# Attention scores from quarters of the array, x kept in token rows: one change to a fused attention, expert and mixing kernel

## The chip, the cores and the metric

The kernel runs on one core of a Trainium2 chip. The metric is the device time of one execution in microseconds (us); lower is better. Engine names: PE is TensorE (matmuls; PEld its weight loads), DVE is VectorE, ACT is ScalarE, POOL is GpSimd, SP is SyncE, which issues nearly all DMAs here.

## What is computed

Three layers run one after another on two sequences of 768 tokens. The change lies in the first. Its reference, cut to what matters:

```python
B, H, S, D = 2, 8, 768, 64                       # block 32, window 16
k_sum = k.reshape(B, H, 24, 32, D).max(axis=3)   # 24 block maxima of k
v_sum = v.reshape(B, H, 24, 32, D).mean(axis=3)  # 24 block means of v
scores_l = scale * (q @ k.T)                     # kept where |i - j| < 16
scores_s = scale * (q @ k_sum.T) + log(32)
a = softmax(concat(masked scores_l, scores_s))
x = a @ concat(v, v_sum)                         # then (B, S, H * D)
```

Then each token is sent to one of 8 experts (512 to 1024 to 512, the choice partly carried over from the token before), and a last layer mixes tokens and channels.

## The kernel before, in words

**Units.** Heads are taken in pairs: n = 0..7 is a pair of a batch (four pairs to a batch). Queries are taken in windows of 64 tokens; window t needs the 96 keys around it and the 24 block maxima, KC = 120 columns. A unit k = 3n + g is four windows of one pair, so there are 24 units, k0 to k23. `units` is run by one loop (L907), whose body writes each engine's order out by hand; nothing is reordered later.

**One unit.** `attn_s` (L238) makes the scores: four fp32 matmuls of 128 rows by 128 columns, each over 120 moving columns. The 128 rows hold 64 channels of each of the two heads, and the stationary operand is `qb`, in which q stands twice on a diagonal with zeros elsewhere, so that the first 64 outputs belong to head 0 and the last 64 to head 1. `q_diag` (L207) copies q into it, on POOL for every pair but the first. Each fp32 matmul appears in the trace as two passes. The scores of a unit fill one PSUM bank of `sps`, with two banks in turn. DVE then adds the mask and takes the row minimum (L248, four instructions and their accumulator reads), and ACT takes the exponential (L250). In the next turn of the loop `attn_t` (L254) transposes the four results on PE, ACT copies them out (L258), later `attn_v` (L260) multiplies them with v in 64-column halves, and `attn_n` (L271) divides on DVE.

**Operands.** `ka[n]` holds the 120 score columns: `k_windows` (L218) copies the overlapping windows, `k_max` (L227) makes the block maxima on DVE and copies them to all 12 windows. For n = 0 ACT and DVE do this, for n = 1 DVE, then POOL. `kc[n]`, `qf[n]` and `vall` come by DMA in the order in which SP issues them; `kc` has two buffers, `qf` borrows two buffers of the expert stage. `vsum` (L174) makes the block means of v: matmuls at k3, k5 and k6 (batch 0), a copy by ACT (L181), a matmul (L184), a copy of one window by ACT (L192), and then POOL spreads it over the other 11 windows (L193, L195). The first `attn_v` stands in k9 and needs them.

**Behind the attention.** From k12 the finished rows of x are stored (`store_x`, L280) and transposed for the gate (`gate_T`, L288, L298; ACT copies them out, L304). In k17 the gate of batch 0 is computed (L316), and from k18 to k23 the routing of batch 0 (`route0`) runs in small DVE steps between the attention's, with some PE hops (L322, L350, L355, L371, L454). Then come the end of batch 1, the first gather of tokens and the expert layers (from L633), and from about 249 us the mixing layer.

The columns of x stand with all even heads first (`xs` is [64 h + i, window, pair, channel]), and the host permutes the rows of the gate's and the experts' first weights to match.

Of the kernel before, what the change touches and what calls it, by code (L numbers as in the profile page):

```python
# [10 lines left out]
F32 = mybir.dt.float32  # L11
F32R = mybir.dt.float32r
# [5 lines left out]
ALU = mybir.AluOpType  # L18
AX = mybir.AxisListType
PSUM = bass.MemoryType.PSUM  # L20
DRAM = bass.MemoryType.DRAM

B, H, S, D = 2, 8, 768, 64
NP = H // 2
NT = S // 64
DM = 512
E = 8
DFF = 1024
W = 96
NB = 24  # L30
KC = W + NB
D1 = D + 1
# [3 lines left out]
TS = 256  # L36
# [19 lines left out]
def consts():  # L56
    import numpy as np

    c = np.zeros((128, C_N), np.float32)
    p = np.arange(128)  # L60
    c[:, C_W8:C_W8 + 8] = 8 - np.arange(8)
    c[:, C_I128:C_I128 + 128] = np.arange(128)
    c[:, C_I26:C_I26 + 26] = np.arange(26)
    c[:, C_TOK:C_TOK + 12] = 128 * np.arange(12)[None, :] + p[:, None] + 1
    c[:, C_PAD:C_PAD + 30] = B * S + 1 + 128 * np.arange(30)[None, :] + p[:, None]
    s = 128 * np.arange(6)[None, :] + p[:, None]
    c[:, C_KEY:C_KEY + 6] = 16 * (s + 1)
    c[:, C_S0:C_S0 + 6] = s == 0
    c[:, C_TRI:C_TRI + 128] = p[:, None] < p[None, :]
    for x in range(3):  # L70
        c[16:48, C_IND + 34 * x] = 1.0 / 32
        c[48:80, C_IND + 34 * x + 1] = 1.0 / 32
    c[:, C_I13:C_I13 + 13] = np.arange(13)
    for x in range(4):
        for j in range(6):
            c[32 * x + j, C_PRM + 6 * x + j] = 1.0
    m = np.full((128, 3, KC), -1.0e9, np.float32)
    i = p % 64
    j = np.arange(W)
    band = np.abs(j[None, :] - 16 - i[:, None]) < 16  # L80
    for v, (lo, hi) in enumerate(((16, W), (0, W), (0, W - 16))):
        ok = band & (j >= lo)[None, :] & (j < hi)[None, :]
        m[:, v, :W][ok] = 0.0
        m[:, v, W:] = 8.0 * math.log(32.0)
    return c, m.reshape(128, 3 * KC)
# [3 lines left out]
def tile_attn_moe_mix(ctx: ExitStack, tc: tile.TileContext, qT, kT, vp, gw, w1, w2, wth, wtok, wch, cst, msk, out):  # L89
    nc = tc.nc  # L90
    V, A, G, T, SP = nc.vector, nc.scalar, nc.gpsimd, nc.tensor, nc.sync

    def pool(name, bufs, stack=ctx, **kw):
        kw.setdefault("reuse_waits", "tile")
        return stack.enter_context(tc.tile_pool(name=name, bufs=bufs, **kw))
# [3 lines left out]
    xd = dram.tile([B * S, DM], F32, name="xd")  # L99
# [5 lines left out]
    idn = const.tile([128, 128], F32, name="idn")  # L105
# [39 lines left out]
    xp = pool("xp", 1, sA)  # L145
    kp = pool("kp", 2, sA)
    ptp = pool("ptp", 1, sA)
    qp = pool("qp", 1, sA)
    psS = pool("psS", 2, sA, space=PSUM)
    psT = pool("psT", 2, sA, space=PSUM)  # L150
    psO = pool("psO", 2, sA, space=PSUM)

    qb = [qp.tile([128, NT, 128], F32, name=f"qb{i}") for i in range(2)]
    xs = [xp.tile([128, NT, NP, 64], F32, name=f"xs{1 - b}") for b in range(B)][::-1]
    ka, kcs = {}, {}
    qf = {}

# [8 lines left out]
    def vslot(b, g):  # L166
        return (3 * b + g) % NVS
# [33 lines left out]

    def load_q(n):
        b, p = divmod(n, NP)
        qf[n] = xt_p.tile([128, 4, TS], F32R, name="qf", tag="xl" if n % 2 else "xh").bitcast(F32).rearrange("p c t -> p (c t)")[:, 0:S]
        SP.dma_start(qf[n], qT[b, 2 * p:2 * p + 2].rearrange("h d s -> (h d) s"))

    def q_diag(n, lo, hi):  # L207
        for h in range(2):
            dst = qb[n % 2][64 * h:64 * h + 64, lo:hi, 64 * h:64 * h + 64]
            src = qf[n][64 * h:64 * h + 64].rearrange("p (t i) -> p t i", i=64)[:, lo:hi, :]  # L210
            if n > 0:
                G.tensor_copy(dst, src)
            elif h == 0:
                A.copy(dst, src)  # L214
            else:
                V.tensor_copy(dst, src)

    def k_windows(n):  # L218
        kc = kcs[n]
        ka[n] = kp.tile([128, NT, KC], F32, name="ka", tag="ka")  # L220
        win = bass.AP(tensor=kc.tensor, offset=kc.offset, ap=[list(kc.ap[0]), [64, NT], [1, W]])
        if n == 0:
            A.copy(ka[n][:, :, 0:W], win)
        else:
            (V if n < 2 else G).tensor_copy(ka[n][:, :, 0:W], win)

    def k_max(n, lo, hi):  # L227
        if lo == 0:
            kss[n] = st.tile([128, NB], F32, name="ks", tag="ks", bufs=2)
        V.tensor_reduce(kss[n].rearrange("p (c x r) -> p x c r", c=4, x=3)[:, lo:hi],  # L230
                        kcs[n][:, 16 + 256 * lo:16 + 256 * hi].rearrange("p (x c r j) -> p x c r j", c=4, r=2, j=32),
                        axis=AX.X, op=ALU.max)
        if hi == 3:
            (V if n < 2 else G).tensor_copy(ka[n][:, :, W:KC], kss.pop(n).unsqueeze(1).to_broadcast([128, NT, NB]))

    kss = {}

    def attn_s(n, g):  # L238
        sps = psS.tile([128, 4, KC], F32, name="sps", tag="s")
        for c in range(4):  # L240
            t = 4 * g + c
            T.matmul(sps[:, c, :], qb[n % 2][:, t, :], ka[n][:, t, :], start=True, stop=True)  # L242
        neg = sp.tile([128, 4, KC], F32, name="neg", tag="neg")
        mn = st.tile([128, 4], F32, name="mn", tag="mn")
        for c in range(4):
            t = 4 * g + c
            v = 0 if t == 0 else (2 if t == NT - 1 else 1)
            V.tensor_tensor_reduce(out=neg[:, c, :], in0=sps[:, c, :], in1=mk[:, v, :], scale=-0.125, scalar=3.0e38,  # L248
                                   op0=ALU.add, op1=ALU.min, accum_out=mn[:, c:c + 1])
            A.activation(neg[:, c, :], neg[:, c, :], AF.Exp, bias=mn[:, c:c + 1], scale=-1.0)  # L250
            micro(1)
        return neg
# [7 lines left out]
    def attn_v(k):  # L260
        n, g = units[k]
        b, p = divmod(n, NP)
        ops = psO.tile([128, 4, D1], F32, name="ops", tag="o")
        for c in range(4):
            for h in range(2):
                hd = 2 * p + h
                T.matmul(ops[64 * h:64 * h + 64, c, :], ptl[k][:, c, 64 * h:64 * h + 64],
                         vall[0:KC + 1, vslot(b, g), c, D1 * hd:D1 * hd + D1], start=True, stop=True)
        return ops

    def attn_n(k, ops):  # L271
        n, g = units[k]
        b, p = divmod(n, NP)
        ri = st.tile([128, 4, 1], F32, name="ri", tag="ri")
        V.reciprocal(ri, ops[:, :, D:D1])
        micro()
        V.tensor_tensor(xs[b][:, 4 * g:4 * g + 4, p, :], ops[:, :, 0:D], ri.to_broadcast([128, 4, D]), op=ALU.mult)
        micro()

    def store_x(b, g):  # L280
        for h in range(2):
            SP.dma_start(
                xd[b * S + 256 * g:b * S + 256 * g + 256, 256 * h:256 * h + 256].rearrange("(t i) c -> i t c", i=64),
                xs[b][64 * h:64 * h + 64, 4 * g:4 * g + 4].rearrange("i t p d -> i t (p d)"))

    xT = {}

    def gate_T(b, g2, tail=False):  # L288
        if g2 % 2 == 0:
            xT[b, g2 // 2] = wsp.tile([128, 1024], F32R, name="xT", tag="whi" if g2 == 4 else "wlo").bitcast(F32).rearrange("p (c t) -> p c t", c=4)  # L290
        if tail and g2 % 2:
            ps = psT.tile([128, 4, 128], F32, name="psx", tag="t")
        else:
            ps = psM.tile([128, 4, 128], F32, name="psx", tag="m")
        pv = ps.rearrange("p (h g) (t i) -> p h g t i", h=2, t=2)
        for tt in range(2):
            for g in range(2):
                T.transpose(pv[:, :, g, tt, :], xs[b][:, 2 * g2 + tt, 2 * g:2 * g + 2, :], idn)  # L298
        o = 128 * (g2 % 2)
        dst = xT[b, g2 // 2][:, :, o:o + 128]  # L300
        if tail and g2 % 2:
            V.tensor_copy(dst, ps)
        else:
            A.copy(dst, ps)  # L304
# [511 lines left out]
        return next(gen, "end")  # L816


    G.memset(qb[0], 0.0)
    V.memset(one, 1.0)  # L820
    V.memset(qb[1], 0.0)
    load_k(0)
    load_q(0)
    SP.dma_start(mk, msk.rearrange("p (a j) -> p a j", a=3))
# [19 lines left out]
    warm = psM.tile([128, 128], F32, name="warm", tag="m")  # L844
    for x in range(NWARM):
        T.matmul(warm, one, one, start=x == 0, stop=x == NWARM - 1)
    k_windows(0)
    k_max(0, 0, 3)
    q_diag(0, 0, 4)
    q_diag(0, 4, NT)  # L850

    def advance():
        r = state["tok"] = step(state["bg"])
# [53 lines left out]
    for k in range(NG + 8):  # L907
# [6 lines left out]
        if k < NG:  # L914
            n, g = units[k]
            cur = attn_s(n, g)
            if n + 1 < B * NP:
                if g == 0:
                    k_windows(n + 1)
                    k_max(n + 1, 0, 1)  # L920
                elif g == 1:
                    k_max(n + 1, 1, 3)
            if g == 0 and n + 1 < B * NP:
                q_diag(n + 1, 0, NT)
            if g == 0 and 0 < n < B * NP - 2:
                load_k(n + 2)
                load_q(n + 2)
# [552 lines left out]
```

## Time and profile before

| | us |
|---|---|
| three runs | 431.9, 435.61, 435.96 |
| median | 435.61 |
| the profiled execution, its own time | 431.91 |
| its span in the trace | 430.1 |
| PE busy | 411.0 (96%) |
| PE weight loads busy | 353.8 (82%) |
| DVE busy | 309.5 (72%) |
| ACT busy | 230.9 (54%) |
| POOL busy | 118.4 (28%) |

The span is the stretch that the trace covers; some 1.8 us of the execution's time lie around it. A busy share is a mean over stages with different limits, and matmuls overlap, so that a PE shown busy need not be at its peak. The attention takes about the first 76 us of the span.

### The profile page before, as it was taken

The numbers are of one execution on the slowest core, as the hardware profiler recorded it, in microseconds if no ns is written. First come the engines' busy times: TensorE is split into PE (matmuls) and PEld (weight loads), VectorE is DVE, ScalarE is ACT, GpSimd is POOL, SyncE is SP. The second block draws the span as 40 slices with busy tenths as digits, with TensorE's granted clock in tenths as the row PEclk, the third lists the DMA queues.
The fourth block names the chain that finished last, engine by engine and source line by source line (L and its number), as shares of the span: only waits on it lengthen the run. The fifth ranks groups of instructions, "written<-read, shape, count | busy, mean of one in ns | idle before, by whom it ended". The sixth has DMA issues, their size and how long they took to land.

```text
span 430.1 us, 7952 instructions
## 1 busy us (share of the span) xinstructions
PE 411.0 (96%) x2917; PEld 353.8 (82%) x2917; DVE 309.5 (72%) x737; ACT 230.9 (54%) x424; POOL 118.4 (28%) x108
## 2 busy tenths in 40 slices
PE   8999998799899999999998899999999999999993
PEld 7677877688798989898987788888888788899883
DVE  7575668688897968987899578797988843622731
ACT  5873866645566757775678566564654421211300
POOL 8293732610122105040211121343334710100000
PEclk9999999999999999999999999999999999999998
DMA  8992984984787978989587362322300010100022
GB/s 289 409 391 79 255 263 148 339 307 139 262 269 238 337 244 271 334 261 328 191 299 243 128 231 83 104 74 84 112 26 8 28 40 24 50 13 27 12 75 80
DMA packets 45072, 76.31 MB, mean 177 GB/s; under 512 B 3424, under 2 KB 28256, under 8 KB 44256
## 3 DMA queue, kind: packets, MB, share of 16 engines
q1 hardware_dynamic: 42944, 68.89, 47.9%
q0 software_dynamic: 2080, 6.82, 4.2%
q8 instruction: 25, 0.41, 0.4%
q14 instruction: 23, 0.19, 0.1%
HBM read 62.85 MB, written 12.85 MB: 176 GB/s over the span
## 4 chain that ended last, share of the span: by engine, by line
PE 42%; ACT 3%; DVE 3%; DMA 1%; issue 1%; ACTq 0%
PE ya L1240 15%; PE yb L1240 8%; PE pth L1178 8%; PE psch L1265 8%; DVE wlo L596 1%; DMA wraw<-in_w_dram 1%; PE psxt L1115 1%; ACT whi L595 1%; PE psy L685 1%; PE pl L743 0%; ACT dg L772 0%; ACT dl L773 0%; DVE hl L639 0%; PE yb L1231 0%; DVE dg L776 0%
## 5 line engine op out<-in xcount | busy, mean ns | idle before, releaser
L596 DVE TENSOR_TENSOR wlo<-wraw,whi 128x1024 fp32r<-128x1024 f32 x53 | 64.4, 1219 | 14.0 <-ACT whi L595 14.0
L595 ACT CAST whi<-wraw 128x1024 fp32r<-128x1024 f32 x56 | 58.1, 1046 | 4.5 <-DMA wraw<-in_w_dram 3.3
L751 POOL DMA_INDIRECT yd<-y,ixs x13 | 17.0, 1307 | 118.9 <-ACT y L711 98.4
L250 ACT ACTIVATE neg<-neg,mn 128x120 f32<-128x120 f32 x96 | 30.2, 385 | 22.1 <-DVE mn L248 21.4
L633 PE MATMUL psh<-xl,whi 128*128 128x256 f32 x192 | 31.2, 284 | 2.0 <-DVE xl L619 1.9
L1208 POOL TENSOR_TENSOR r<-r,x 128x512 f32<-128x512 f32 x10 | 13.0, 1304 | 69.9 <-ACT r L1203 69.9
L633 PE MATMUL psh<-xh,whi 128*128 128x256 f32 x192 | 31.4, 285 | 0.6 <-DVE hl L639 0.6
L633 PE MATMUL psh<-xh,wlo 128*128 128x256 f32 x192 | 30.8, 283 | 0.0
L248 DVE CUSTOM_DVE_ANT_0 neg<-sps,mk 128x120 f32<-128x120 f32 x96 | 21.7, 278 | 12.5 <-PE tps L257 5.8
L704 PE MATMUL psy<-whi,hh 128*128 128x512 f32 x96 | 30.7, 401 | 0.0
L704 PE MATMUL psy<-wlo,hh 128*128 128x512 f32 x96 | 29.8, 392 | 0.0
L704 PE MATMUL psy<-whi,hl 128*128 128x512 f32 x96 | 29.8, 392 | 0.0
L633 PEld LDWEIGHTS psh<-xl,whi 128*128 128x128 f32 x192 | 26.5, 191 | 2.4 <-DVE xl L619 2.4
L633 PEld LDWEIGHTS psh<-xh,whi 128*128 128x128 f32 x192 | 26.6, 191 | 1.6 <-DVE hl L639 0.8
L242 PEld LDWEIGHTS sps<-ka,qb 128*128 128x128 f32 x192 | 23.7, 195 | 4.7 <-DVE mn L248 1.7
L242 PE MATMUL sps<-ka,qb 128*128 128x120 f32 x192 | 27.1, 286 | 0.2 <-ACT qb L214 0.2
L633 PEld LDWEIGHTS psh<-xh,wlo 128*128 128x128 f32 x192 | 26.5, 192 | 0.0
L772 ACT ACTIVATE dg<-raw 128x768 f32<-128x768 f32 (+1 forms) x20 | 16.3, 817 | 18.7 <-issue 3.7
L1271 DVE SCALAR_TENSOR_TENSOR o<-psch,xTr 128x512 f32<-128x512 f32 (+1 forms) x8 | 4.4, 552 | 28.7 <-PE psch L1265 28.7
L638 ACT ACTIVATE hh<-psh 128x512 fp32r<-128x512 f32 x24 | 14.3, 595 | 14.9 <-PE psh L633 14.8
L604 POOL DMA_INDIRECT xg<-xd,ixg x13 | 15.5, 1195 | 21.5 <-DVE ip L413 10.5
L704 PEld LDWEIGHTS psy<-whi,hl 128*128 128x128 f32 x96 | 18.0, 188 | 4.0
(462 smaller groups left out, 1151.3 us busy)
## 6 DMA issues: line engine op xcount, KB each, us to landing
wraw<-in_w_dram SPq DMA_DIRECT2D x56, 512.0 KB, 4.9
raw<-in_wtok_dram SPq DMA_DIRECT2D x12, 768.0 KB, 6.8
vall<-in_v_dram SPq DMA_DIRECT2D x6, 1040.0 KB, 9.0
kc<-in_k_dram SPq DMA_DIRECT2D x8, 400.0 KB, 6.0
qf<-in_q_dram SPq DMA_DIRECT2D x8, 384.0 KB, 6.7
xd<-xs SPq DMA_DIRECT2D x12, 256.0 KB, 5.4
yd<-zro SPq DMA_DIRECT2D x6, 512.0 KB, 6.4
x<-yd SPq DMA_DIRECT2D x12, 256.0 KB, 2.7
```

What stands on the lines that cost most here:

```text
L242: T.matmul(sps[:, c, :], qb[n % 2][:, t, :], ka[n][:, t, :], start=True, stop=True)
L248: V.tensor_tensor_reduce(out=neg[:, c, :], in0=sps[:, c, :], in1=mk[:, v, :], scale=-0.125, scalar=3.0e38, op0=ALU.add, op1=ALU.min, accum ...
L250: A.activation(neg[:, c, :], neg[:, c, :], AF.Exp, bias=mn[:, c:c + 1], scale=-1.0)
L595: A.copy(hi, r)
L596: (G if j == 0 and q < 3 else V).tensor_tensor(lo, r, hi.bitcast(F32), op=ALU.subtract)
L633: T.matmul(ps[:, mm, :], a[:, c, fs], x[:, c, :], start=n == 0, stop=n == 11)
L704: T.matmul(ps, a[:, f, ts_], w[:, f, :], start=q == 0 and n == 0, stop=q == 3 and n == 5)
L751: G.indirect_dma_start(out=yd, out_offset=bass.IndirectOffsetOnAxis(ap=ixs[:, c:c + 1], axis=0), in_=ysb[j, r], in_offset=None)
L772: A.activation(g, hw.bitcast(F32), AF.Copy, scale=2.0 ** -112)
L1178: T.matmul(pt[:, cs_], a[:, c, :], wthp[c][wi][:, cs_], start=n == 0, stop=n == 11)
L1240: T.matmul(ps, a[:, ms], w[:, t], start=part == 0 and ii == 0 and n == 0, stop=ii == 5 and n == 5 and (part == 0 or m % 2 == 1))
L1265: T.matmul(ps, wchp[c][wi][:, ms], x[:, c, t], start=n == 0, stop=n == 11)
```

## The change

The scores of a unit come from 16 smaller blocks' worth of array: for each pair of windows there are four matmuls of 64 rows by 64 columns, one for each combination of head (rows) and window (columns), and q goes in as it was loaded. Rows of a score tile are now the 128 tokens of two windows of one head. The scores of head 0 go to one PSUM bank and those of head 1 to another; a unit uses 240 columns of both banks, and the next unit the other 240 columns of the same two banks. `qb`, its memsets and `q_diag` are gone; `qf` has three buffers of its own. `attn_v` and `attn_n` follow the new rows with as many instructions as before. x has tokens in its partitions, so that a store is one DMA with rows of 2 KB instead of two with pieces of 1 KB, a gate transpose takes a plain 128-column slice, and the weights are no longer permuted. The windows of pair 0 are copied in two pieces on ACT, and for pair 1 windows and block maxima are copied by POOL instead of DVE.

```diff
+    sps = psS.tile([128, 2, 512], F32, name="sps")        # psS: bufs 2 -> 1
-        qf[n] = xt_p.tile(...)[:, 0:S]
+        qf[n] = qp.tile([128, S], F32, name="qf", tag="qf")    # 3 buffers
-    def q_diag(n, lo, hi):
-            if n > 0:
-                G.tensor_copy(dst, src)
...
-            (V if n < 2 else G).tensor_copy(ka[n][:, :, 0:W], win)
+            G.tensor_copy(dst, win)
...
     def attn_s(n, g):
-        sps = psS.tile([128, 4, KC], F32, name="sps", tag="s")
-        for c in range(4):
-            t = 4 * g + c
-            T.matmul(sps[:, c, :], qb[n % 2][:, t, :], ka[n][:, t, :], start=True, stop=True)
+        x = (3 * n + g) % 2
+        ps = [[sps[:, h, 240 * x + 120 * a:240 * x + 120 * a + KC] for a in range(2)] for h in range(2)]
+        for a in range(2):
+            for r in range(2):
+                for h in range(2):
+                    t = 4 * g + 2 * a + r
+                    hs_ = slice(64 * h, 64 * h + 64)
+                    T.matmul(ps[h][a][64 * r:64 * r + 64, :], qf[n][hs_, 64 * t:64 * t + 64], ka[n][hs_, t, :],
+                             start=True, stop=True)
...
     def store_x(b, g):
-        for h in range(2):
-            SP.dma_start(xd[...256 * h:256 * h + 256]..., xs[b][64 * h:64 * h + 64, 4 * g:4 * g + 4]...)
+        SP.dma_start(xd[b * S + 256 * g:b * S + 256 * g + 256, :].rearrange("(a p) c -> p a c", p=128),
+                     xs[b][:, 2 * g:2 * g + 2])
...
-    G.memset(qb[0], 0.0)
-    V.memset(qb[1], 0.0)
-    k_windows(0)
+    k_windows(0, 0, 4)
     k_max(0, 0, 3)
-    q_diag(0, 0, 4)
-    q_diag(0, 4, NT)
+    k_windows(0, 4, NT)
...
-            if g == 0 and n + 1 < B * NP:
-                q_diag(n + 1, 0, NT)
```

## Rows read from the trace of the kernel before

**Rows 1.** Busy time by stretch: stretch, length, busy us (instructions), PE clock, DMA share, GB/s.

```profile
6.00:25.00 19.00, 18.93 (x131) 13.06 (x131) 11.81 (x76) 14.21 (x42) 9.81 (x14) 1.00 1.03 412
25.00:54.00 29.00, 28.19 (x387) 22.37 (x388) 18.87 (x107) 18.29 (x51) 19.46 (x18) 1.00 0.69 219
54.00:76.00 22.00, 20.19 (x272) 16.93 (x272) 16.87 (x111) 14.33 (x40) 5.54 (x7) 1.00 0.67 209
```

**Rows 2.** PE's waits, 0 to 90 us: total, times, longest.

```profile
PE ops L267 <- DVE ri L275: 0.5, 1, 0.5
```

**Rows 3.** PE's waits, 90 us to the end.

```profile
PE psh L633 <- DVE xl L619: 1.9, 1, 1.9
```

**Rows 4.** Timeline around the scores of k10, k14, k16: start, length, instructions.

```profile
28.78 1.15 PE L242 MATMUL sps<-ka,qb 128*128 128x120 f32 x8
29.86 0.69 PE L267 MATMUL ops<-vall,pt 121*64 121x65 f32 x16
30.07 0.28 DVE L248 CUSTOM_DVE_ANT_0 neg<-sps,mk 128x120 f32<-128x120 f32 x1 [0.54 <-PE sps L242]
30.48 0.65 PE L257 MATMUL tps<-idn,neg 128*120 128x128 f32 x4
...
44.82 1.15 PE L242 MATMUL sps<-ka,qb 128*128 128x120 f32 x8
45.81 0.60 PE L298 MATMUL psx<-idn,xs 128*128 128x128 f32 x4
...
50.95 1.05 PE L242 MATMUL sps<-ka,qb 128*128 128x120 f32 x8
51.84 0.60 PE L298 MATMUL psx<-idn,xs 128*128 128x128 f32 x4
```

**Rows 5.** Timeline, block means of v: four 32-column groups, then one 24-column group.

```profile
13.09 1.07 PE L179 MATMUL pv<-vall,ind 96*32 96x512 f32 x8
...
43.23 1.04 PE L184 MATMUL pvb<-sv,ind 128*24 128x512 f32 x2
```

**Rows 6.** Timeline, 19 to 27 us: what k6 to k9 wait for.

```profile
19.85 0.16 PEld L179 LDWEIGHTS pv<-vall,ind 96*32 96x32 f32 x8 [0.24 <-DMA vall<-in_v_dram]
...
21.59 0.42 DVE L230 TENSOR_REDUCE ks<-kc 128x8 f32<-128x256 f32 x1 [1.13 <-DMA kc<-in_k_dram]
...
24.21 0.58 ACT L192 COPY vall<-pvb 24x512 f32<-24x512 f32 x1
...
24.95 1.47 POOL L193 COPY vall<-vall 24x1536 f32<-24x1536 f32 x1
...
26.47 0.43 PEld L267 LDWEIGHTS ops<-vall,pt 121*64 121x64 f32 x12 [0.25 <-POOL vall L193]
```

**Rows 7.** ACT and the gate, k15 to k17: one stretch, then timeline.

```profile
47.12:50.95 3.83, 3.64 (x54) 3.22 (x53) 2.09 (x13) 3.81 (x11) 3.82 (x3) 1.00 0.98 264
...
54.57 0.59 ACT L304 COPY xT<-psx 128x512 f32<-128x512 f32 x1
54.90 2.23 PE L316 MATMUL psg<-xT,wg 128*32 128x256 f32 x24
```

**Rows 8.** POOL and DVE in the routing, k18: timeline, then the stretch of k19.

```profile
58.55 1.70 POOL L212 COPY qb<-qf 64x768 f32<-64x768 f32 x2
59.31 0.20 DVE L338 TENSOR_TENSOR eq<-lg,m 128x48 f32<-128x48 f32 x1
59.76 0.55 DVE L340 TENSOR_TENSOR eq<-eq,cs 128x48 f32<-128x48 f32 x1
...
61.36:63.91 2.55, 2.55 (x33) 2.18 (x32) 2.52 (x15) 2.14 (x8) 0.00 (x0) 1.00 0.34 101
```

**Rows 9.** Timeline, last unit: k23's scores, k22's last accumulator read, k23's first reduction.

```profile
71.65 1.13 PE L242 MATMUL sps<-ka,qb 128*128 128x120 f32 x8
72.17 0.08 DVE L248 DVE_READ_ACCUMULATOR2_ANT mn<- 128x1 f32 x1
72.92 0.28 DVE L248 CUSTOM_DVE_ANT_0 neg<-sps,mk 128x120 f32<-128x120 f32 x1
```

More of the change, by code (lines that the diff above doesn't have):

```diff
@@ L80, in consts @@
     band = np.abs(j[None, :] - 16 - i[:, None]) < 16
-    for v, (lo, hi) in enumerate(((16, W), (0, W), (0, W - 16))):
-        ok = band & (j >= lo)[None, :] & (j < hi)[None, :]
+    for v in range(3):
+        lo = np.where((v == 0) & (p < 64), 16, 0)
+        hi = np.where((v == 2) & (p >= 64), W - 16, W)
+        ok = band & (j[None, :] >= lo[:, None]) & (j[None, :] < hi[:, None])
         m[:, v, :W][ok] = 0.0
@@ L147, in tile_attn_moe_mix @@
     ptp = pool("ptp", 1, sA)
-    qp = pool("qp", 1, sA)
-    psS = pool("psS", 2, sA, space=PSUM)
+    qp = pool("qp", 3, sA)
+    psS = pool("psS", 1, sA, space=PSUM)
     psT = pool("psT", 2, sA, space=PSUM)
     psO = pool("psO", 2, sA, space=PSUM)
-    qb = [qp.tile([128, NT, 128], F32, name=f"qb{i}") for i in range(2)]
-    xs = [xp.tile([128, NT, NP, 64], F32, name=f"xs{1 - b}") for b in range(B)][::-1]
+    sps = psS.tile([128, 2, 512], F32, name="sps")
+    xs = [xp.tile([128, NT // 2, DM], F32, name=f"xs{1 - b}") for b in range(B)][::-1]
     ka, kcs = {}, {}
@@ L203, in load_q, with k_windows @@
         b, p = divmod(n, NP)
-        qf[n] = xt_p.tile([128, 4, TS], F32R, name="qf", tag="xl" if n % 2 else "xh").bitcast(F32).rearrange("p c t -> p (c t)")[:, 0:S]
+        qf[n] = qp.tile([128, S], F32, name="qf", tag="qf")
         SP.dma_start(qf[n], qT[b, 2 * p:2 * p + 2].rearrange("h d s -> (h d) s"))
-    def q_diag(n, lo, hi):
-        for h in range(2):
-            dst = qb[n % 2][64 * h:64 * h + 64, lo:hi, 64 * h:64 * h + 64]
-            src = qf[n][64 * h:64 * h + 64].rearrange("p (t i) -> p t i", i=64)[:, lo:hi, :]
-            if n > 0:
-                G.tensor_copy(dst, src)
[L213 to L218, printed above, removed]
+    def k_windows(n, lo=0, hi=NT):
         kc = kcs[n]
-        ka[n] = kp.tile([128, NT, KC], F32, name="ka", tag="ka")
-        win = bass.AP(tensor=kc.tensor, offset=kc.offset, ap=[list(kc.ap[0]), [64, NT], [1, W]])
+        if lo == 0:
+            ka[n] = kp.tile([128, NT, KC], F32, name="ka", tag="ka")
+        win = bass.AP(tensor=kc.tensor, offset=kc.offset + 64 * lo, ap=[list(kc.ap[0]), [64, hi - lo], [1, W]])
+        dst = ka[n][:, lo:hi, 0:W]
         if n == 0:
-            A.copy(ka[n][:, :, 0:W], win)
+            A.copy(dst, win)
         else:
-            (V if n < 2 else G).tensor_copy(ka[n][:, :, 0:W], win)
+            G.tensor_copy(dst, win)
     def k_max(n, lo, hi):
@@ L233, in k_max @@
         if hi == 3:
-            (V if n < 2 else G).tensor_copy(ka[n][:, :, W:KC], kss.pop(n).unsqueeze(1).to_broadcast([128, NT, NB]))
+            ks = kss.pop(n)
+            for a_, b_ in ((0, 4), (4, NT)) if n == 0 else ((0, NT),):
+                (V if n == 0 else G).tensor_copy(ka[n][:, a_:b_, W:KC], ks.unsqueeze(1).to_broadcast([128, b_ - a_, NB]))
     kss = {}
     def attn_s(n, g):
-        sps = psS.tile([128, 4, KC], F32, name="sps", tag="s")
-        for c in range(4):
-            t = 4 * g + c
-            T.matmul(sps[:, c, :], qb[n % 2][:, t, :], ka[n][:, t, :], start=True, stop=True)
+        x = (3 * n + g) % 2
[7 more added lines that the diff above has]
+                             start=True, stop=True)
         neg = sp.tile([128, 4, KC], F32, name="neg", tag="neg")
@@ L245, in attn_s @@
         for c in range(4):
-            t = 4 * g + c
-            v = 0 if t == 0 else (2 if t == NT - 1 else 1)
-            V.tensor_tensor_reduce(out=neg[:, c, :], in0=sps[:, c, :], in1=mk[:, v, :], scale=-0.125, scalar=3.0e38,
+            a, h = divmod(c, 2)
+            t = 2 * g + a
+            v = 0 if t == 0 else (2 if t == NT // 2 - 1 else 1)
+            V.tensor_tensor_reduce(out=neg[:, c, :], in0=ps[h][a], in1=mk[:, v, :], scale=-0.125, scalar=3.0e38,
                                    op0=ALU.add, op1=ALU.min, accum_out=mn[:, c:c + 1])
@@ L264, in attn_v @@
         for c in range(4):
[L265 to L268, printed above, removed]
+            a, h = divmod(c, 2)
+            hd = 2 * p + h
+            for r in range(2):
+                T.matmul(ops[64 * r:64 * r + 64, c, :], ptl[k][:, c, 64 * r:64 * r + 64],
+                         vall[0:KC + 1, vslot(b, g), 2 * a + r, D1 * hd:D1 * hd + D1], start=True, stop=True)
         return ops
@@ L276, in attn_n @@
         micro()
-        V.tensor_tensor(xs[b][:, 4 * g:4 * g + 4, p, :], ops[:, :, 0:D], ri.to_broadcast([128, 4, D]), op=ALU.mult)
+        V.tensor_tensor(xs[b][:, 2 * g:2 * g + 2, 128 * p:128 * p + 128].rearrange("p a (h d) -> p a h d", h=2),
+                        ops.rearrange("p (a h) d -> p a h d", h=2)[:, :, :, 0:D],
+                        ri.rearrange("p (a h) x -> p a h x", h=2).to_broadcast([128, 2, 2, D]), op=ALU.mult)
         micro()
     def store_x(b, g):
[L281 to L284, printed above, removed]
+        SP.dma_start(xd[b * S + 256 * g:b * S + 256 * g + 256, :].rearrange("(a p) c -> p a c", p=128),
+                     xs[b][:, 2 * g:2 * g + 2])
     xT = {}
@@ L294, in gate_T @@
             ps = psM.tile([128, 4, 128], F32, name="psx", tag="m")
[L295 to L298, printed above, removed]
+        for c in range(4):
+            T.transpose(ps[:, c, :], xs[b][:, g2, 128 * c:128 * c + 128], idn)
         o = 128 * (g2 % 2)
@@ L1429 @@
     from concourse.bass_utils import run_bass_kernel_spmd as _run
-    def perm(w):
-        n = w.shape[-1]
-        lead = w.shape[:-2]
-        k = len(lead)
-        w = w.reshape(lead + (NP, 2, D, n))
-        return w.transpose(tuple(range(k)) + (k + 1, k, k + 2, k + 3)).reshape(lead + (DM, n))
     def bits(w):
@@ L1459 @@
     gw = _np.zeros((DM, 32), _np.float32)
-    gw[:, 0:E] = perm(inputs["moe_w_gate"])
-    gw[:, E:E + 1] = perm(inputs["moe_w_local"])
+    gw[:, 0:E] = inputs["moe_w_gate"]
+    gw[:, E:E + 1] = inputs["moe_w_local"]
     c, m = consts()
     wtok = _np.stack([inputs["moe2_w_tok_r"].T, inputs["moe2_w_tok_i"].T])
-    ins = [("q", q.transpose(0, 1, 3, 2)), ("k", kp), ("v", vw), ("gw", gw), ("w1", perm(inputs["moe_w1"])),
+    ins = [("q", q.transpose(0, 1, 3, 2)), ("k", kp), ("v", vw), ("gw", gw), ("w1", inputs["moe_w1"]),
            ("w2", inputs["moe_w2"]), ("wth", bits(inputs["moe2_w_theta"])), ("wtok", bits(wtok)), ("wch", bits(inputs["moe2_w_ch"])),
```

## The prediction

> **What bounds the kernel now.** I read the stretches of the attention first, then PE's waits, then the timeline at the places that a shorter score block would move. PE is shown busy 18.93 of 19.00 us up to k8, 28.19 of 29.00 in k9 to k17 and 20.19 of 22.00 in k18 to k23 [rows 1]. The waits say how much of that is real: between 25 and 54 us the longest wait of PE on another engine is 0.5 us [rows 2], and behind 90 us the longest single one is 1.9 [rows 3]. So PE's program order sets the pace, and the expert and mixing layers behind, which the change leaves alone, shift as a block with the end of the attention. But three other things stand close behind PE. Up to k8 the DMA engines are full (share 1.03 [rows 1]). In k15 ACT is busy 3.81 of 3.83 us [rows 7]. In the routing DVE is busy 2.52 of 2.55 us [rows 8]. What PE saves counts only where none of these takes over.
>
> **The scores on PE, the term that is meant.** Before, a unit has four matmuls of two passes each, 8 passes. Between transposes of full width, the scores of k16 hold PE from 50.95 to 51.84, 0.89 us, or 0.11 a pass. In k14, with a 64-column product before, they hold it 0.99 (44.82 to 45.81), and in k10, with such products on both sides, 1.08 (28.78 to 29.86) [rows 4]. So each change between array shapes costs about 0.10.
>
> After, a unit has eight matmuls, 16 passes, each of a quarter of the array over the same 120 columns. How many run side by side decides. Columns do: four 32-column groups with 8 passes of 512 columns last 1.07 us, and one group with 2 such passes 1.04 [rows 5]. Halves by rows are in no row of before. The bounds: four side by side give 4 passes in turn, 0.45 us; columns alone give 8, 0.89; none gives 16, 1.78. I take four, since what the trace shows of columns is full overlap, with a score of each head in its own bank. A quarter shape differs from both neighbours, so two changes are paid everywhere: 0.45 + 0.20 = 0.65 us. A unit then saves 0.43 (1.08 - 0.65) in k10 and k11, 0.34 (0.99 - 0.65) in k12 to k14, and 0.24 (0.89 - 0.65) where transposes stand on both sides. If rows don't overlap, the block is 0.89 + 0.20 = 1.09 and loses 0 to 0.20.
>
> The Trainium skill, "TensorE: Matmul & The Clock Gate", Part 3, says that blocks in different row groups run concurrently as those in column groups do; no run here shows it yet for rows. By it the block is the 0.65 that I take.
>
> **Up to k9: the saving is not kept.** The last transfer of v for batch 0 lands at 19.85, and PE stands for it in k6. The keys of pair 3 land at 21.59, and DVE, which runs in order, stands 1.13 us for them ahead of k7's reductions [rows 6]. Both are in a full DMA stream whose bytes and order don't change. SP can issue some of them earlier, as the third q no longer waits for a borrowed buffer; but a stream that is full doesn't deliver earlier. Behind k7's reductions follow its exponentials, ACT's copy of the block means at 24.21, POOL's spread at 24.95 (1.47 us) and k9's product, which waits for POOL until 26.47 [rows 6]. Removing `q_diag` from POOL doesn't help, because POOL is ahead of that copy. k7 can start its reductions right behind the 0.42 us of L230 that began at 21.59 [rows 6] instead of behind PE, about 0.1 us. Gain at k9's product: 0.1. The memsets, the diagonal copies of pair 0 and the work moved from DVE to POOL for pair 1 all lie ahead of 19.85 and cost or give nothing for the same reason; without that cover, the moved window copy would be one POOL operation of about the spread's 1.47.
>
> **k9 to k17: kept until ACT is full.** PE saves 2 x 0.43 + 3 x 0.34 = 1.9 in k10 to k14. k15 to k17 would add 3 x 0.24 = 0.7, but there ACT hands on: exponentials, copies out and gate copies without a pause in k15, and the last gate copy at 54.57 ends (0.59 us long) behind the start of the gate at 54.90 [rows 7]. ACT's run starts from k14's scores, which are ready 1.5 (k10 to k13) + 0.45 earlier, some 2.0 us. PE alone would bring the gate 2.6 forward, ACT 2.0; I take 2.3.
>
> **k18 to k23: the routing.** Shorter scores give nothing where DVE has no pause. But DVE loses something to POOL there: while POOL runs `q_diag` from 58.55 for 1.70 us, DVE's L340 takes 0.55, against 0.20 for L338 of the same shape [rows 8]. Without `q_diag` that 0.35 comes back, and L335 beside it may give some more: 0.3 to 0.6, I take 0.5.
>
> **The wait that the change adds.** All units now use the same two banks. A unit's first reduction starts at 30.07, 0.14 behind the end of all 8 passes (28.78 + 1.15) [rows 4], though its own columns were done earlier: users of a bank are kept apart. So the next unit's scores must wait until the last reduction has left the banks. Behind these scores on PE are the transposes of the unit before, and then DVE. Mostly other work fills the gap: a 64-column product and transposes (29.86 to beyond 31) [rows 4]. In k23 it shows: scores began at 71.65, while k22's last read ends at 72.25 (72.17 + 0.08) [rows 9]. They start 0.6 later, are 0.45 shorter, and so k23's first reduction (72.92) comes 0.15 later. In k8 and k9 the same wait ends before POOL's spread. Cost: 0.15, and at most 0.15 in each of six routing units, 0.9.
>
> The Trainium skill, "PSUM — Partial Sum Buffer", on bank collisions, speaks against this layout: TensorE writing a bank while another engine reads it must be kept apart by bank, whatever the columns. The trace agrees (0.14 behind the last pass).
>
> The store of x has as many bytes in half as many DMAs, and nothing waits for it in the shown stretches: 0. Gate transposes, products and divisions keep their counts and sizes: 0.
>
> **Sum.** 0.1 + 2.3 + 0.5 - 0.15 = 2.75 us. The profiled execution took 431.9 (span 430.1 and 1.8 around it), which gives 429.1. It is the lowest of three runs (431.9 to 435.96), and the median is 435.61; carried over to the median the change gives 432.8.
>
> **Rivals.**
> - Early part freed: if v and the keys of pair 3 land earlier, the part up to k9 gives at most what PE saves there, nine units of 0.34, 3.1 us, beside the 2.75. With half of it the total is 4.3, 431.3 on the median; with all of it 5.9, 429.7. For it: SP issues the third q, and the v behind it, earlier. Against it: DMA share 1.03.
> - Row halves don't overlap: the block is 1.09, the units k10 to k17 lose 0 to 0.20 each (some 0.5 to 0.8 before ACT hides part), against 0.6 won elsewhere: 435.5, no change. For it: no row of before has two row halves at once.
> - On the other side, quarters one after another: 1.78 + 0.20 = 1.98 us a block, 0.9 to 1.1 more in each unit. PE is at its limit in k10 to k17, so 8 us there, some 4 more in the routing and perhaps 5 in the early part: 435.6 + 17, about 452. It decides as soon as a block takes more than about 1.35 us: 0.35 over the mean block of 1.0, in the 8 units k10 to k17, is 2.8 and eats the whole gain. Against it: columns overlap in full [rows 5].
> - The bank wait is paid in full in each routing unit: 2.75 - 0.75 = 2.0, 433.6; within my case.
>
> **How the numbers follow.** My forecast (quarters overlap, early part held by DMA): 0.60. Early part freed: 0.17. No overlap of rows: 0.15. Quarters one after another or a wait I don't see: 0.08. A measurement of this kernel can tell about 1% from no change, 4.4 us; my forecast lies within it, but the runs shown are spread over 4 us, and a median may fall at either end. So of my case a quarter comes out as faster by over 1% (0.15) and most of the early case (0.15): faster 0.30. Same: 0.45 of my case, the rest of the early case and most of the no-overlap one, 0.60. Slower: 0.10. My case's own range is 430 to 435. The range that holds eight in ten goes from 427 (early part freed, at the low end of the runs) to 437.5 (no overlap, at the high end), and leaves the serial case out.
>
> **What would show it.** Right: the score blocks hold PE about 0.65 us, with the passes of a block starting nearly together in fours; v and the keys of pair 3 land as before, near 19.8 and 21.5; the gate starts near 52.5; L340 takes about 0.20; k23's scores start right behind k22's last read; everything from 90 us on is the same, shifted. Wrong: blocks of 1 us or more, landings that moved, or the gate earlier by more than 3 us.

## The result and the profile after

The changed kernel's median is 430.25 us in 20 runs (426.41 to 431.33), against 434.29 in 20 runs of the kernel before on the same chips (430.76 to 435.96): ratio 0.9902, 95% interval 0.9883 to 0.9922. That is about 4.0 us of gain; 432.8 and a gain of 2.75 were forecast. The profiled execution took 431.33 us (span 429.5) and is the longest of the 20.

| us | before | after |
|---|---|---|
| profiled execution | 431.91 | 431.33 |
| its span | 430.1 | 429.5 |
| PE busy | 411.0 | 404.9 |
| DVE busy | 309.5 | 305.2 |
| POOL busy | 118.4 | 106.4 |

The stretches of [rows 1], after (stretch, length, busy us of PE, PEld, DVE, ACT and POOL with instructions, granted PE clock, DMA share, GB/s):

```profile
6.00:25.00 19.00, 14.26 (x210) 7.70 (x202) 11.05 (x78) 15.22 (x44) 5.30 (x7) 1.00 1.03 411
25.00:54.00 29.00, 27.55 (x482) 19.01 (x475) 19.47 (x109) 20.17 (x56) 15.55 (x13) 1.00 0.79 272
54.00:76.00 22.00, 18.88 (x316) 14.62 (x315) 17.98 (x108) 15.03 (x37) 5.47 (x5) 1.00 0.61 201
```

Up to 25 us PE is busy 14.26 us instead of 18.93, and the DMA engines are as full as before (1.03): the saving has become idle time. PE's waits of 0 to 90 us name what it stands for now (total, times, longest; the view of [rows 2]). The first, the bank wait, and the third, v's transfers, are not among before's waits; the second was 2.2 us there:

```profile
PE sps L241 <- DVE mn L249: 2.1, 4, 0.7
PE psi L484 <- DVE rh L480: 1.6, 1, 1.6
...
PE pv L181 <- DMA vall<-in_v_dram: 1.5, 2, 1.0
```

The timeline after, at the places of [rows 4, 6, 7, 8, 9] (start, length, instructions, idle time before and its releaser):

```profile
19.59 1.07 PE L181 MATMUL pv<-vall,ind 96*32 96x512 f32 x8 [0.48 <-DMA vall<-in_v_dram]
21.34 0.42 DVE L223 TENSOR_REDUCE ks<-kc 128x8 f32<-128x256 f32 x1 [1.74 <-DMA kc<-in_k_dram]
...
25.95 0.68 PE L269 MATMUL ops<-vall,pt 121*64 121x65 f32 x14 [0.52 <-POOL vall L195]
...
28.23 0.64 PE L241 MATMUL sps<-ka,qf 64*64 64x120 f32 x16
28.80 0.69 PE L269 MATMUL ops<-vall,pt 121*64 121x65 f32 x16
...
48.28 0.64 PE L241 MATMUL sps<-ka,qf 64*64 64x120 f32 x16
48.85 0.66 PE L298 MATMUL psx<-idn,xs 128*128 128x128 f32 x4
...
51.52 0.59 ACT L304 COPY xT<-psx 128x512 f32<-128x512 f32 x1
51.65 2.42 PE L316 MATMUL psg<-xT,wg 128*32 128x256 f32 x24
...
55.52 0.64 PE L241 MATMUL sps<-ka,qf 64*64 64x120 f32 x16
...
56.57 0.20 DVE L340 TENSOR_TENSOR eq<-eq,cs 128x48 f32<-128x48 f32 x1
...
67.66 0.29 PE L454 MATMUL psi<-rh,loh 128*128 128x2 f16 x6 [0.56 <-DVE rh L450]
...
68.32 0.08 DVE L249 DVE_READ_ACCUMULATOR2_ANT mn<- 128x1 f32 x1
...
68.46 0.64 PE L241 MATMUL sps<-ka,qf 64*64 64x120 f32 x16 [0.51 <-DVE mn L249]
...
69.27 0.28 DVE L249 CUSTOM_DVE_ANT_0 neg<-sps,mk 128x120 f32<-128x120 f32 x1
```

Two more lines of before's timeline, the scores of k18 and the first index product of the routing:

```profile
58.48 1.08 PE L242 MATMUL sps<-ka,qb 128*128 128x120 f32 x8
...
71.50 0.29 PE L454 MATMUL psi<-rh,loh 128*128 128x2 f16 x6 [0.81 <-DVE rh L450]
```

A score block now holds PE 0.57 us (28.23 to 28.80, 48.28 to 48.85), beside narrow products and beside transposes; it was 1.08, 0.99 or 0.89 [rows 4]. In the trace's single records the 16 passes of k10 start in four groups of four, 7 ns apart within a group, the groups 0.15, 0.10 and 0.10 us apart. v and the keys land a quarter of a us earlier than in [rows 6], the gate starts at 51.65 instead of 54.90 [rows 7], and L340 takes 0.20 instead of 0.55 [rows 8].

The profiled execution shows only 0.6 us of gain because TensorE's clock fell twice in it, to the lower of its two levels (1.2 instead of 2.4 GHz), behind the waits of lines 484 and 633. A stretch at the lower level is called a half-clock stretch below. Stretches after (columns as above):

```profile
83.70:87.10 3.40, 3.40 (x19) 3.40 (x18) 2.25 (x11) 0.57 (x2) 1.62 (x2) 0.50 0.90 339
...
110.75:114.42 3.67, 3.67 (x16) 3.37 (x17) 2.28 (x3) 1.57 (x3) 0.00 (x0) 0.54 0.93 354
```

In the profiled execution of before there is no such stretch from 7 to 427 us. So single spans can't be compared; sections can. From the traces of all kernels (number of half-clock stretches between 72 and 420 us; scores of k10; from there to the scores of k18; from there to the first index product, L454; from there to the end of the span):

| profile | half-clock | k10 at | k10 to k18 | to L454 | to the end |
|---|---|---|---|---|---|
| before | 0 | 28.78 | 29.70 | 13.02 | 358.56 |
| before, again (e_before) | 1 | 28.19 | 29.69 | 13.20 | 361.00 |
| before, idle matmuls (e_befill) | 0 | 28.48 | 29.70 | 13.20 | 358.70 |
| before, one bank (e_onebank) | 1 | 31.64 | 29.68 | 12.86 | 359.44 |
| after | 2 | 28.23 | 27.29 | 12.14 | 361.80 |
| after, again (e_after) | 2 | 28.42 | 27.29 | 12.14 | 361.33 |
| after, heads outermost (e_heads) | 0 | 28.34 | 27.44 | 12.14 | 357.97 |
| after, copies of q (e_qdiag) | 1 | 29.52 | 27.30 | 12.21 | 360.21 |
| after, pair 1 on DVE (e_pair1) | 1 | 28.32 | 27.28 | 12.14 | 360.41 |
| after, idle matmuls, some behind the wait (e_fill) | 1 | 31.03 | 27.29 | 12.14 | 360.29 |
| after, idle matmuls (e_fill4) | 0 | 29.14 | 27.31 | 12.14 | 358.24 |
| after, more of them (e_fill5) | 0 | 28.55 | 27.42 | 12.14 | 358.07 |
| after, one row half (e_rows) | 1 | 44.25 | 29.93 | 12.77 | 359.70 |
| after, one row half, idle matmuls (e_rowsfill) | 2 | 46.02 | 29.91 | 12.78 | 361.29 |

The two middle columns repeat within 0.2 us where the score layout and its banks are the same. They hold most of the gain: 2.41 + 0.88 = 3.29 us, or 3.47 with the 13.20 that two repeats of before take to L454. The last column is about 0.5 shorter after where no stretch fell (358.56 and 358.70 against 357.97 to 358.24); no run shows why, and x in token rows was not tried by itself. One or two stretches add 0.8 to 3.8 us to it.

### The profile page after: what moved, and what is told of

Read it like the earlier page. It is cut to its first block, busy times and chain, and to the rows that moved or that the text cites. A ratio compares the mean times of both kernels' runs of the same rounds, so it can differ in the third digit from the quotient of the medians.

```text
span 429.5 us, 8298 instructions
## 1 busy us (share of the span) xinstructions
PE 404.9 (94%) x3109; PEld 343.1 (80%) x3109; DVE 305.2 (71%) x733; ACT 230.9 (54%) x423; POOL 106.4 (25%) x95
## 5 line engine op out<-in xcount | busy, mean ns | idle before, releaser
L633 PE MATMUL psh<-xl,whi 128*128 128x256 f32 x192 | 32.3, 291 | 1.9 <-DVE xl L619 1.9
L633 PE MATMUL psh<-xh,whi 128*128 128x256 f32 x192 | 32.5, 293 | 0.6 <-DVE hl L639 0.6
L633 PE MATMUL psh<-xh,wlo 128*128 128x256 f32 x192 | 31.7, 288 | 0.0
L633 PEld LDWEIGHTS psh<-xl,whi 128*128 128x128 f32 x192 | 27.5, 198 | 2.4 <-DVE xl L619 2.4
L633 PEld LDWEIGHTS psh<-xh,whi 128*128 128x128 f32 x192 | 27.7, 199 | 1.7 <-DVE hl L639 0.8
L633 PEld LDWEIGHTS psh<-xh,wlo 128*128 128x128 f32 x192 | 27.4, 198 | 0.0
L639 DVE SCALAR_TENSOR_TENSOR hl<-psh,hh 128x512 fp32r<-128x512 f32 x24 | 16.5, 687 | 8.9 <-ACT hh L638 8.7
L704 PEld LDWEIGHTS psy<-wlo,hh 128*128 128x128 f32 x96 | 18.0, 188 | 3.9
```

The source lines that it names most:

```text
L633: T.matmul(ps[:, mm, :], a[:, c, fs], x[:, c, :], start=n == 0, stop=n == 11)
L639: V.scalar_tensor_tensor(hl, ps, 0.0, hh.bitcast(F32), op0=ALU.max, op1=ALU.subtract)
L704: T.matmul(ps, a[:, f, ts_], w[:, f, :], start=q == 0 and n == 0, stop=q == 3 and n == 5)
```

## The experiments

The theory: the gain is the score block on PE, because both its row halves and its column halves run side by side. Rivals: POOL and DVE, freed of copies, carry it; or the early part; or a clock that differs.

**The kernel before, again** (e_before).

> The kernel before, unchanged, against itself: what its executions show of TensorE's granted clock. If the spread of its runs (431 to 436 us) is stretches at half clock, executions with a mean clock near 0.996 lie near 431, and each further 0.004 of mean clock lost goes with about 1.7 us more. If the spread has another cause, time and clock don't go together.

Measured: 433.90 against 433.90, ratio 1.0016 (0.9995 to 1.0037). Two copies of one kernel agree within 0.4%, but in the profiled one the clock fell once, from 113.77 to 117.18 us. Time and clock go together only in part: the run with the highest mean clock, 0.995, took 433.39 where about 431 was expected, and one at 0.989 took 432.92. So half-clock stretches are not the whole of the spread.

**Heads outermost** (e_heads): all of head 0's matmuls are written ahead of head 1's.

```diff
-        for a in range(2):
-            for r in range(2):
-                for h in range(2):
+        for h in range(2):
+            for a in range(2):
+                for r in range(2):
```

> The kernel after with the loop over heads outermost, so that the row halves of the array come one after another and only the column halves side by side. Theory 'row overlap carries it': a score block goes from 0.57 us to about 0.57 + 4 x 0.105 = 0.99, the gate of batch 0 starts 2 to 3 us later than after's 51.65, and the time is 2 to 3 us above after's, near 432.5 to 433.5 beside a before of 434.3. Rival 'the POOL copies carried it': block length doesn't matter, within 0.7 us of after (430.3).

Measured: 430.12, ratio 0.9915 (0.9882 to 0.9949), blocks of 0.58 to 0.59 where PE does not wait behind them. The passes still start in fours (k10: 28.343, .350, .370, .376), so the two heads still run together, and the run doesn't tell the theories apart. Whether TensorE or the build brought the second head forward stays open. The Trainium skill, "TensorE: Matmul & The Clock Gate", Part 3, has matmuls start strictly in the order of the program; if the build keeps the written order, these starts speak against it.

**Both heads in one row half** (e_rows), where nothing can run beside it by rows.

```diff
-                    hs_ = slice(64 * h, 64 * h + 64)
+                    hs_ = slice(0, 64)
```

> Head 1's score matmuls read rows 0 to 63 of q and keys too, so its scores are those of head 0; everything else is as in the changed kernel. All 16 passes then lie in the upper half of the rows, and only two of them (the two column halves) can run side by side. Theory (the gain of k9 to k17 is the overlap of the two row halves): four groups of passes 0.10 us apart plus 0.16 us make the 0.57 us of the changed kernel, so eight groups make about 0.97; the gate product of the first sequence starts 2 to 3.5 us later than in the changed kernel (51.65), and the time is 432 to 433.5 us. Rival (the gain comes from GpSimd and VectorE, freed of copies, and the block does not matter): the block is longer, but the gate product stays within 0.5 us of 51.65 and the time within 0.5 us of the changed kernel's.

Its timeline, k10 and the gate:

```profile
44.25 1.09 PE L241 MATMUL sps<-ka,qf 64*64 64x120 f32 x16
45.27 0.69 PE L269 MATMUL ops<-vall,pt 121*64 121x65 f32 x16
...
70.78 1.95 PE L316 MATMUL psg<-xT,wg 128*32 128x256 f32 x24
```

The block holds PE 1.02 us, and its passes start in eight pairs, most of them 0.10 us apart. From k10's scores to the gate it takes 26.53 us, against 23.42 after and 26.11 before; to k18 29.93, against 27.29 and 29.70. So the overlap of the row halves is the gain from k10 to k18: without it nothing of the 2.41 is left, although all else of the change, x in token rows too, is still there. The same part of the Trainium skill (Part 3 of "TensorE: Matmul & The Clock Gate") has blocks in different row groups run concurrently; the trace agrees, fours against pairs.

The time was a miss: three of the four runs took 447.77 to 448.53 (median of all 447.89) instead of 432 to 433.5, the fourth 435.55. In the profiled one (448.53) the scores of k10 come 16 us late, and the clock stands at half from 9.99 to 44.12 us. The same stretch of e_rows and of before:

```profile
10.00:40.00 30.00, 29.37 (x182) 18.03 (x182) 9.16 (x65) 14.95 (x42) 7.39 (x8) 0.50 0.71 260
```

```profile
10.00:40.00 30.00, 29.32 (x319) 20.61 (x321) 18.56 (x115) 19.85 (x58) 18.14 (x19) 1.00 0.83 325
```

PE is shown as busy in the one as in the other; the clock is 0.50 in the one and 1.00 in the other. A score block of that stretch holds PE 1.85 us, those from k10 on 1.02. The three long runs have a mean clock of 0.954; the fourth has 0.988, which leaves no room for 34 us at half. So most of the 16 us goes with the clock, and row halves in turn do not bring it down in every run.

**The same with idle matmuls** (e_rowsfill; 128 by 128, of a constant tile, their result is not used), to hold the clock up.

```diff
+        if 1 <= k < 9:
+            f2 = psO.tile(...)[:, 0:128]
+            m = 14 if k == 5 else 6
+            for x in range(m):
+                T.matmul(f2, one, one, start=x == 0, stop=x == m - 1)
```

> Head 1's scores from rows 0 to 63, as in the run with both heads in the upper half (its scores are those of head 0), with the same idle matmuls in units k1 to k8. Theory (in that run the 13 us beyond the block's price came from the clock, which stood at half from 10 to 44 us): full clock in the early part, the scores of k10 at 28.5 to 30.5 us, k10 to k18 again 29.9 us, and a median of 432.5 to 434.5 us, that is 2.5 to 4 us over the changed kernel. Rival (the serial row halves hold the early part by themselves): the scores of k10 stay behind 35 us and the time above 440 us.

Measured: 444.63 (437.42 to 451.87); in the profiled run, the longest, the scores of k10 stand at 46.02. The stretch again:

```profile
10.00:40.00 30.00, 30.00 (x197) 19.47 (x194) 8.01 (x55) 12.84 (x36) 3.59 (x6) 0.50 0.63 236
```

A miss: in that run the clock fell at 9.48 all the same and stood at half until 40.20. Here too the time goes with the mean clock, from 437.42 at 0.994 to 451.87 at 0.954. What brings the clock down in some runs and not in others is open. The sections behind k10 repeat those of e_rows (29.91 and 12.78).

**One score bank before** (e_onebank): the new wait on the old, long blocks.

```diff
-    psS = pool("psS", 2, sA, space=PSUM)
+    psS = pool("psS", 1, sA, space=PSUM)
```

> The kernel before with one PSUM bank for the scores instead of two: the added wait alone, on long score blocks. Theory 'the wait lies under other work': next scores start 0.06 to 0.2 us behind the last reduction in about ten units, and the time is 0 to 1.5 us above before. Rival 'the wait costs in full': 0.9 us (0.88 block after the reductions) in most of 24 units, 5 us or more above before.

Measured: 436.22 against 433.90, ratio 1.0081 (1.0048 to 1.0114), between the two expectations. PE's waits up to 30 us:

```profile
PE sps L242 <- DVE mn L248: 2.7, 4, 0.8
```

The loss lies ahead of k10, whose scores start at 31.64 instead of 28.19 to 28.78; behind, the sections are those of before. No wait of PE for a load is left in that stretch. Up to k9 a unit's scores, DVE's reads and the next unit's scores follow one another, so with blocks of 1 us this chain, and not the loads, seems to set the pace; that is argued from the waits. In the changed kernel the chain has the same links (the wait of 2.1 us above) but blocks of 0.57, and k10 isn't later.

**The copies of q, put back** (e_qdiag), into a tile that nobody reads.

```diff
+                for h_ in range(2):
+                    G.tensor_copy(dg_[64 * h_:64 * h_ + 64], qf[n + 1][64 * h_:64 * h_ + 64])
```

> The changed kernel with the diagonal copies of q back on GpSimd (two of 64x768 for each pair after the first), into a scratch tile that nothing reads. Theory (the copies cost 0.5 us by slowing VectorE's small operations in the routing, nothing else): the two small operations of lines 335 and 340 go back from 0.16 and 0.20 us to about 0.34 and 0.55, the index product of line 484 starts about 0.5 us later relative to the scores of k18 than in the changed kernel, and the scores of k10 to k17 stay where they are. Rival (GpSimd was a bound between 25 and 54 us, and its copies delayed windows and spreads): the scores of k12 and k15 move later by more than 0.5 us and most of the 4 us is lost.

```profile
54.21 1.71 POOL L924 COPY dgq<-qf 64x768 f32<-64x768 f32 x2
```

```profile
57.87 0.20 DVE L342 TENSOR_TENSOR eq<-eq,cs 128x48 f32<-128x48 f32 x1
```

Measured: 431.01 in one run, k10 to k18 27.30, to L454 12.21. POOL's time for the copies costs nothing there, so this rival falls. The other half of the expectation wasn't tested: the last copies end at 55.92, ahead of L342 (L340 after), since their tile waits for no scores, and the small operation keeps its 0.20. The routing says it better: e_onebank still has its copies, but there they end at 61.83, just ahead of the small operations (61.89 on). Its L340 takes 0.20 and its routing 12.86, against 13.02 and 13.20 in before and e_before, where L340 takes 0.55. So by L454 the collision costs 0.16 to 0.34 us, if e_onebank's new wait costs nothing in that stretch.

**Pair 1 back on DVE** (e_pair1).

```diff
-            G.tensor_copy(dst, win)
+            (V if n < 2 else G).tensor_copy(dst, win)
```

> The changed kernel with the windows and the spread block maxima of pair 1 back on VectorE. Theory (this part of the change is off the path): the scores of k3 to k9 and the product that waits for the spread of v(0,2) stay within 0.15 us of the changed kernel's (25.95 us). Rival (this is what brings the product 0.5 us earlier than before): it goes back to about 26.4 us.

```profile
26.04 0.68 PE L269 MATMUL ops<-vall,pt 121*64 121x65 f32 x14 [0.53 <-POOL vall L195]
```

Measured: 430.01 in one run; the product that waits for the spread resumes at 26.04 instead of 25.95. This part of the change is off the path.

**Idle matmuls in the waits** (e_fill, e_fill4, e_fill5, e_befill), and the changed kernel beside them (e_after).

> The kernel after with idle matmuls (bf16, 128 columns, result unused) in PE's two longest waits of the first expert passes: 24 ahead of L484's wait near 82 us, 28 in L633's wait near 109 us. Theory 'half-clock stretches follow these waits': no stretch at half clock at 84 and 111 us, mean clock near 0.995, time near 427 (after 430.3 less two times 1.7). Rival 'the clock falls for another reason': stretches stay, time 430 to 431.

Measured: 429.65, ratio 0.9908 (0.9880 to 0.9937), and not near 427. The 28 at L633 did not start in the wait (1.87 us) but behind it, since their buffer was still being read. The clock stayed up at both places all the same and fell at others, from 17.45 to 24.28 and from 75.48 to 78.89.

e_fill4 writes them to a buffer that is free, and adds 14 ahead of the first transposes of gathered tokens:

```diff
+        if (j, q, mm) == (1, 0, 0):
+            for x in range(28):
+                T.matmul(ps[:, 1, 0:128], one, one, start=x == 0, stop=x == 27)
```

> The changed kernel with idle 128x128 matmuls ahead of three long waits of TensorE: 14 ahead of the first transposes of gathered tokens, 24 ahead of line 484, 28 ahead of the first hidden layer of the second expert group. Theory (a part idle TensorE is what the half-clock stretches follow, and they make the 4 us between single runs): no half-clock stretch behind 76 us in its profile, and the median falls from 430.3 to about 427 to 428.5. Rival (the stretches come whatever TensorE does in these waits): the median stays at 430 to 431, with stretches elsewhere.

Measured: 428.16 (427.34 to 431.85), ratio 0.9885 (0.9819 to 0.9952), full clock from 4 to 424 us in the profile.

> The changed kernel once more, beside the two with idle matmuls, as their common base. Both theories expect 430 us (426.5 to 431.5 in single runs), a profile in which the scores of k10 to those of k18 take 27.3 us, and single half-clock stretches at places that differ from run to run.

> The idle matmuls of the run before (14, 24 and 28 ahead of the three long waits), and 6 of 128x128 in each of the units k1 to k8 (14 in k5) where TensorE waits for loads. Theory (half-clock stretches follow a lightly used TensorE, and idle matmuls keep the clock up): no half-clock stretch in its profile, median 426.5 to 428.5 and at least 1.5 us under the changed kernel in the same call; the scores of k10 start at 28.2 to 29.2 us as before. Rival (the fill of the early units is paid for, since each unit's scores follow the fourth operation of the last one by 0.1 us in half of the units): the scores of k10 start 1 to 2 us later and the median is that of the changed kernel or worse.

Measured beside the same runs of before: e_after 430.46 (428.65 to 431.01), ratio 0.9915 (0.9882 to 0.9947), with half-clock stretches at the places where the first profile had them (from 83.31 and 110.62); not at other places, as expected. e_fill5, which adds the early units' idle matmuls shown above: 428.02 (427.75 to 430.22), ratio 0.9880 (0.9840 to 0.9920), and the stretch behind L484 at full clock:

```profile
83.70:87.10 3.40, 3.40 (x31) 3.40 (x31) 3.19 (x18) 1.54 (x2) 1.92 (x2) 1.00 1.04 399
```

> The kernel before with the same idle matmuls ahead of the three long waits behind the attention (14, 24 and 28), none in the early units. Theory A (the change is worth 2.4 us from k10 to k18 and about 0.9 us in the routing behind it, 3.3 in all, and the clock does the rest to both kernels alike): no half-clock stretch in the profile, the scores of k10 to those of k18 take 29.7 us, median 431 to 432.2 us, that is 3 to 4 us over the 428.0 to 428.2 of the filled changed kernel. Theory B (much of the 4 us between the kernels is the clock): the median comes to 429 to 430.5, within 2.5 us of the filled changed kernel.

Measured: 431.56 (430.83 to 433.22), ratio 0.9940 (0.9918 to 0.9963), full clock to 427 us. By medians, idle matmuls bring the kernel before 2.6 us (434.17 to 431.56) and the changed one 2.4 (430.46 to 428.02). So the clock takes about as much from both kernels, as far as these runs tell, and with the clock held up the change is worth 431.56 - 428.02 = 3.5 us. The two were measured on different chips; their ratios to before there, 0.9940 and 0.9880, put it at 2.6, some 2 us either way. The sections of the two profiles are sharper: 29.70 - 27.42 = 2.28, 13.20 - 12.14 = 1.06 and 358.70 - 358.07 = 0.63, 4.0 in all. The fastest version run is e_fill5; its lead over e_fill4 (0.14 us) is no difference.

## Why the prediction was right, and where its terms were off

The time (432.8 forecast, 430.25 measured) lies in the range and the mechanism is the one named, but the gain was put at 2.75 us and is 3.5 to 4.0. The other 1.3 us between 432.8 and 430.25 are no gain: the forecast counted from 435.61, the median of the three runs shown, and 20 runs of before have 434.29. Point by point:

- **The score block.** Four side by side is right. 0.65 was too long: 0.57 was measured. The four groups and the step to the next operation are all there is; the two changes between array shapes, put at 0.10 each, cost 0.12 together beyond the 0.45 of four passes.
- **Up to k9: nothing kept** (0.1). Right. After's k10 starts 0.55 earlier than before's, and the gate by 3.25 in all, which the prediction had named as a sign against it. But before itself starts k10 anywhere from 28.19 to 28.78, and the changed kernel from 28.23 to 29.14 at full clock with the early part unaltered (after, e_fill4). The 0.55 lies within that scatter; 0.25 of it is in the landings of v and the keys.
- **k9 to k17, 2.3.** Measured 2.41 from k10 to k18, but from other terms. Blocks of 0.57 save 0.51 in k10 and k11, 0.42 in k12 to k14 and 0.32 in k15 to k17: 3.2 us, of which 0.8 isn't kept. Up to k15's scores (47.12 before, 44.56 after) 2.01 of 2.28 is kept, behind them 0.40 of 0.96. ACT does hand on, as forecast: it is busy 3.70 of 3.72 us in k15 (line below, after), its last gate copy ends at 52.11 (51.52 + 0.59), 23.88 us behind k10's scores instead of 26.38 (54.57 + 0.59 - 28.78), and the gate, begun ahead of that copy's end, waits for it. So the chain on ACT keeps 2.50.

```profile
44.56:48.28 3.72, 3.34 (x61) 2.70 (x61) 2.19 (x13) 3.70 (x11) 3.72 (x3) 1.00 1.16 367
```

- **The routing, 0.5 from POOL's copies.** The sign is right and the cause mostly another. From k18's scores to L454 0.88 was gained (1.06 against the repeats of before). Where the copies collide, their price is about right: the first small product behind L340, L350, stands 2.77 to 2.94 us behind k18's scores with the collision and 2.20 without (2.22 in e_rows), 0.55 to 0.74 less. But by L454 only 0.16 to 0.43 of that is left (12.86 in e_onebank and 12.77 in e_rows, against 13.02 and 13.20). The rest is the block: without overlap of rows, and with no copies, that stretch takes 12.77 (e_rows), with it 12.14. The step that failed is "shorter scores give nothing where DVE has no pause": the routing's own small products stand behind the score blocks in PE's order. L355, right behind k19's block, comes 3.52 behind k18's scores in e_rows and 3.15 after; and DVE waits for such products: at L420 0.4 us in e_rows, 0.2 before, none after.
- **The bank wait, 0.15.** Right. k23's scores start at 68.46, 0.06 behind k22's last read (68.32 + 0.08). They stand 0.80 behind L454 instead of 0.15 (71.65 - 71.50), 0.65 later where 0.6 was forecast, and their first reduction 1.61 behind it instead of 1.42, 0.19 later. That the wait stays this cheap hangs on the short block, which the prediction did not say: with long blocks the same wait takes 3 us of the early part (e_onebank).
- **Rivals.** Row halves that don't overlap were put at 435.5; e_rows gives back 2.64 us from k10 to k18 and 0.63 in the routing, as that rival had it. The one run of e_rows with a mean clock of 0.988 took 435.55, where the rival had 435.5, no more than a hint from one run; the clock that fell in the others it did not see. Early part freed: no. Quarters one after another: no.
- **Behind 90 us "the same, shifted".** Nearly, in undisturbed traces (0.5 shorter); but each profile of the plain kernels has zero to two half-clock stretches there, and what they add is as large as the forecast gain. No term stood for it.

## What to carry to other kernels

Two products that share a full-width matmul only by zeros beside a diagonal belong in separate quarters of the array: here that takes 36 to 47% off PE's time for them (0.57 instead of 0.89 to 1.08 us) and saves the copies that build the diagonal. Price a shorter block in every stage where other steps queue behind it on that engine, and see which engine takes over: ACT kept a quarter of the saving. Before a gain of 1% is read from a span, look at the granted clock and compare the sections between two fixed instructions.

## What was not expected of the hardware

- TensorE's clock fell to 0.50 for 3.41 us at a time behind the waits of L484 or L633 in seven of nine profiles of kernels without idle matmuls, and a single stretch behind 72 us goes with a last column that is 0.8 to 2.4 us longer. In three profiles with idle matmuls well placed there was none. A wait alone does not decide it. Ahead of L484, before's PE stands 2.19 us and the clock stays; after's stands 1.64 and it falls, in both profiles, but with 1.58 in e_heads and 1.59 in e_pair1 it stays. Ahead of L633 PE stands 1.87 in before and in e_before, and the clock falls in the second alone. Why is open.
- In the early part a short half-clock stretch costs nothing that shows: e_heads had one from 9.69 to 13.11 and e_pair1 from 10.00 to 13.41, and their k10 starts at 28.34 and 28.32. Longer ones do not seem to be free: with 6.83 us at half, from 11.91 in e_qdiag and from 17.45 in e_fill, k10 starts at 29.52 and 31.03 (up to 29.14 at full clock).
- With all scores in one row half the clock stayed at half for 34 us in the profiled run, though not in every run, while PE was shown as busy as before (29.37 and 29.32 of 30 us); with idle matmuls of full width between (30.00) it did so for 31 us. The busy share that a profile shows did not tell which clock was granted.
